# First-chunk products in plain float32, weights loaded ahead of the keys, and zero products in TensorE's idle time

## The chip, the cores and the metric

The kernel runs on one core of a Trainium2 chip. The metric is the device time of one execution in microseconds (us), the median over runs; lower is better. A profile is one further execution, seen by the hardware profiler: its span goes from the first to the last instruction.

## What is computed

A packed attention in float32 (8 batches, 8 heads, 576 positions, 64 columns a head, 32 packed rows) feeds a feed-forward layer with an ELU. The weights `w_in` (512 x 2048) and `w_out` (2048 x 512) come in as float64, everything else as float32.

```python
def sm_attn(qq, kk, vv):
    s = scale * np.matmul(qq, kk.transpose(0, 1, 3, 2))
    s = s - np.max(s, axis=-1, keepdims=True)
    a = np.exp(s)
    a = a / (np.sum(a, axis=-1, keepdims=True) + 1e-09)
    return np.matmul(a, vv)
p_packed = sm_attn(p, k, v)                 # 32 rows a head
attn = sm_attn(q, p_packed, p_packed)       # 576 rows a head
x = attn.transpose(0, 2, 1, 3).reshape(B * S, H * D)
h = x @ w_in
g = np.where(h > 0.0, h, alpha * (np.exp(np.minimum(h, 0.0)) - 1.0))
return (g @ w_out).astype(np.float32)
```

## The kernel before

**Attention, for each batch.** TensorE makes the packed scores (`s1`, L443) from packed rows and keys; VectorE (DVE) takes the maximum (L453), ScalarE (ACT) the exponential with its sum (L467); TensorE transposes it (L498), multiplies it with the values (`pv`, L524) and transposes the normalised result once more (L550), which gives `ppT`, the packed rows in the layout that both later products use. Then, for each half of 288 positions, come the scores of the queries (`s2`, L569) and their softmax over 32 packed rows: two 32 x 32 transposes out of PSUM on DVE (`fold`, L577), maximum (L584), subtraction (L587), exponential on ACT (L593), sum (L597), reciprocal (L600, L603), product (L606) and the transpose back (`unfold`, L612).

**M instead of x.** Instead of x @ w_in, the kernel multiplies `ppT` with `w_in` first: `mstep` (L663) makes M, 256 rows (32 packed rows of 8 heads, in two groups) by 512 columns of d_ff, in two parts of 256 columns for batches 0 and 1, in one for the others. The hidden product (L761) is then M times the softmax `a`.

**Splits.** [...] The splits are: M (`m_hi`, cast at L246; `m_lo`, L673), `a` (`a_hi`, L246; `a_lo`, L620), the ELU result g (`g_hi`, L246; `g_lo`, L798) and the output weights (high at L310, low at L313). L246 is a helper that copies or casts on ACT or DVE. The small products of the attention and M are in unsplit float32.

**Weights.** Each of 16 blocks of `w_in` and 16 of `w_out` (128 columns, or rows, of d_ff; 512 KB as float64) is loaded into one of three raw buffers and turned into float32 with integer and float operations: on DVE L269, L284, L290, L297 and L305, on ACT L276 and L281. A `w_out` block is then split; the first eight live in `wo_a`, the others in `wo_b`, which takes the place of batch 0's temporary buffers once these are free (`home_op`, L727).

**Steps and visits.** A step is a batch, a window of its positions (256 or 320) and one block f of d_ff: the hidden product (L761, six matmuls), ELU on ACT and DVE (L768, L774, L777), the split, and the output products (L857, L858, L860), three matmuls of 512 columns for each of two or three tiles of 128 positions, accumulated in PSUM over a visit. The 13 visits of batches 0 and 1 interleave batches and chunks of four blocks, so that few weights are needed early: steps 0 to 3 are batch 0's first window with blocks 0 to 3, steps 4 to 7 its second window, 8 to 11 batch 1's first (320 positions; three tiles a step, one of which takes 64 positions kept from batch 0), 12 to 15 its second, and step 16 is the first with block 4. Later batches run all 16 blocks at once.

**The order of the work.** Nothing is ordered by hand. `op` records each operation with a priority (mostly the step that needs it, less a lead), its cost on the engines that may do it, the operations it depends on and the buffers it takes or uses. `schedule` (L150 to L197) then plays the program with these costs: in planned time, the operation of the lowest priority number that is ready, has its buffers and finds its engine idle goes next. What is written out is that order, and each engine's queue is then in order, SP's queue of loads too. Priorities come from `T_ATT` (later batches), `T_ATT1` (batch 1), `T_S2` (the second half of batch 0), `LI` and `LO` (leads of the weights), `LM` and `TM` (M) and `LOOK` (how many steps the output products follow the hidden ones). PSUM is eight banks, held one by one or in aligned pairs (`Banks`, L101); s1, transposes, pv, s2 and M take pairs; hidden products and accumulators take single ones. At most two hidden products are open at a time (ring `h`), and keys, values and queries of later batches share two buffers in `kvq`.

Batch 0 loads first (packed rows 64 KB, keys 1152 KB, values 1152 KB, queries 1152 KB), then the first two blocks of `w_in` and one of `w_out`.

Of the kernel before, what the change touches and what calls it, by code (L numbers as in the profile page):

```python
# [20 lines left out]
def packed_attention_elu_ffn(  # L21
# [128 lines left out]
    def schedule():  # L150
# [19 lines left out]
        while todo:  # L170
# [21 lines left out]
            else:  # L192
# [3 lines left out]
                now = min(ends)  # L196
        return out  # L197

# [19 lines left out]
    warm = const.tile([P, 1], F32, name="warm")  # L218
    nc.scalar.activation(out=warm, in_=ebias, func=AF.Exp, scale=0.0)
    w_in_sb = const.tile([P, NPAIR, DFF], F32, name="w_in_sb")  # L220
    wo_a = const.tile([P, NFA, 2, E], F32R, name="wo_a")
# [7 lines left out]
    R = {k: Ring(n) for k, n in dict(  # L229
        kvq=2, m=NFC, m_late=1, a=2, tmp=3, g=3, e=2, part=2, h=2,  # L230
        raw=3, ex=2, sg=1, mi=2, p=2, ppT=3, pp=1,
    ).items()}
    R["psum"] = Banks(8)

    def banks(n):
        b = Buf(R["psum"], lambda: psum[:, b.at, :] if n == 1 else psum[:, b.at:b.at + n, :], n)
        return b

    def wo(f, part):
# [8 lines left out]

    w_ready, conv_ops = {}, []

    def weights(f, first, prio):
# [47 lines left out]
        def product(e):  # L299
            ms, pw = mi_b.t.bitcast(F32), ex_b.t.bitcast(BF16)  # L300
            out = ms
            if first:
                out = w_in_sb[:, :, f * P:(f + 1) * P]
                ms, pw = (x.rearrange("p (c f) -> p c f", c=NPAIR) for x in (ms, pw))
            nc.vector.scalar_tensor_tensor(  # L305
                out=out, in0=ms, scalar=2.0 ** -20, in1=pw, op0=ALU.mult, op1=ALU.mult
            )

        def high(e):
            copy(e, wo(f, 0), mi_b.t.bitcast(F32))  # L310

        def low(e):
            nc.vector.tensor_tensor(  # L313
                out=wo(f, 1), in0=mi_b.t.bitcast(F32), in1=wo(f, 0).bitcast(F32), op=ALU.subtract
            )
# [7 lines left out]
        g = op(prio, {"DVE": 0.42}, signed, [p, s], use=[ex_b, sg_b])  # L323
        last = op(prio, {"DVE": 0.69}, product, [w, g], use=[mi_b, ex_b])
        if not first:
# [15 lines left out]
    def attention(b, ts):  # L341
# [216 lines left out]
        st.ppT_op = op(ts[3], {"ACT": 0.27, "DVE": 0.29}, tr2c, [o], use=[pt2, st.ppT])  # L558
        st.a_done = []
        prev = []  # L560
        for half in range(2):
            ps = banks(2)
            t1, t2 = temp(), temp()
            mx, sm = {}, {}
# [45 lines left out]

            def unfold(e, t1=t1, t2=t2):
                nc.vector.transpose(out=flat(t2), in_=flat(t1))  # L612

            def hi(e, half=half, t2=t2):
                copy(e, st.a.t[0][:, :, half * HS:(half + 1) * HS],
                     flat(t2).rearrange("p (g s) -> p g s", g=G))

            def lo(e, half=half, t2=t2):
                cs = slice(half * HS, (half + 1) * HS)
                nc.vector.tensor_tensor(  # L620
                    out=st.a.t[1][:, :, cs], in0=flat(t2).rearrange("p (g s) -> p g s", g=G),
                    in1=st.a.t[0][:, :, cs].bitcast(F32), op=ALU.subtract,
                )
# [11 lines left out]
            o = op(t, {"DVE": 0.75}, smul, [o], use=[t1])  # L635
            o = op(t, {"DVE": 0.77}, unfold, [o], take=[t2], use=[t1])
            prev = [o]
            h = op(
                t, {"ACT": 0.67, "DVE": 0.4}, hi, [o] + st.a_done[-1:],
# [7 lines left out]
    def mstep(b, c, part, parts_, prio, deps=()):  # L647
        st = sts[b]
        if part == 0:
            late = b >= NB0 and c == 1  # L650
            st.m[c] = Buf(R["m_late" if late else "m"], lambda: tuple(
                (late_pools["m"] if late else mpool).tile([P, G, FC], F32R, tag=x, name=x)
                for x in ("m_hi", "m_lo")
            ))
        m_b = st.m[c]
# [4 lines left out]
        def mm(e):  # L660
            for pair in range(NPAIR):
                for g in range(G):
# [4 lines left out]
                    )  # L667

        def hi(e):
            copy(e, m_b.t[0][:, :, fs], ps.t[:, :, :w])  # L670

        def lo(e):
            nc.vector.tensor_tensor(  # L673
                out=m_b.t[1][:, :, fs], in0=ps.t[:, :, :w], in1=m_b.t[0][:, :, fs].bitcast(F32),
                op=ALU.subtract,
            )
# [3 lines left out]
        if part:  # L680
            pre.append(st.m_done[c, part - 1])
        o = op(prio, {"PE": 1.0 / parts_ + 0.03}, mm, pre, take=[ps] + ([m_b] if part == 0 else []),
               use=[st.ppT] + ([m_b] if part else []), mode=1)
        h = op(
            prio, {"ACT": 1.02 if parts_ == 1 else 0.58}, hi, [o],
            use=[ps, m_b],
        )
# [31 lines left out]
    for b in range(B):  # L719
# [6 lines left out]
        sts[b] = attention(b, ts)  # L726
    home_op = op(-1000, {"CTL": 0.0}, end_tmp0, sts[0].a_done)  # L727
    for f in range(NF):
# [14 lines left out]
    for i, (b, win, f) in enumerate(order):  # L743
# [10 lines left out]
        ))  # L754
        long = n_tok > 2 * P

        def mm(e, st=st, ps_b=ps_b, m_b=m_b, o=o, cols=cols, n_tok=n_tok):
            n = 0
            for g in range(G):
                for x, y in ((0, 0), (0, 1), (1, 0)):  # L760
                    nc.tensor.matmul(  # L761
                        ps_b.t[:, :n_tok], lhsT=m_b.t[x][:, g, o:o + P], rhs=st.a.t[y][:, g, cols],
                        start=(n == 0), stop=(n == 3 * G - 1),
                    )
                    n += 1
# [39 lines left out]
        def sub_own(e, sub=sub, e_b=e_b, own=own, n_own=n_own):  # L805
# [15 lines left out]
        x4 = op(i, {"DVE": 0.485 if n_own > 256 else 0.415}, elu_own, [x3], use=[e_b, ps_b, h_b])  # L821
        last = []
# [6 lines left out]
        if odd_half:  # L829
# [4 lines left out]
            taker["g"] = y  # L834
            z = op(i, {"DVE": 0.22}, sub_half, [y], use=[g_b])
            half_free[b - 1, f] = [y, z]
            last, taken = [z], []
        y = op(
            i, {"ACT": 0.46 if n_own > 256 else 0.4, "DVE": 0.33 if n_own > 256 else 0.29}, cast,
            [x4] + last, take=taken, use=[e_b] + ([] if taken else [g_b]),  # L840
            after=[taker["g"]] if taken else [],
        )
        taker.update(h=x1, e=x2, g=taker["g"] if odd_half else y)
        z = op(i, {"DVE": 0.48 if n_own > 256 else 0.42}, sub_own, [y], use=[e_b, g_b])
        last.append(z)
# [15 lines left out]

        prev_out = op(
            i + LOOK, {"PE": 0.693 * n_t}, out_mm,
            last + [w_ready[False, f], prev_out],
            take=acc if first else [], use=[g_b] + ([] if first else acc),
        )
        if final:
            t0 = b * S + cols.start
# [63 lines left out]
```

## Time and profile before

| | |
|---|---|
| median of 3 runs | 743.91 us (742.9 to 745.06) |
| profiled execution, its own time | 744.71 us |
| its span | 742.9 us |
| TensorE (PE) busy | 706.4 us, 95% of the span |
| weight loads on TensorE (PEld) | 568.4 us, 77% |
| DVE busy | 512.4 us, 69% |
| ACT busy | 394.5 us, 53% |
| GpSimd (POOL) busy | 19.5 us, 3% |
| mean granted TensorE clock | 0.991 |

The profile lists what each engine did and when, for groups of instructions by source line, and what ended each idle time (the releaser, after an arrow). An operation is written as output tile, arrow, input tiles. Ends of matmuls are modelled and overlap, so the distance between two starts is the better measure in a dense stream. The chain of waits is followed back from the last instruction. The stretches give the busy time of each engine between two moments.

### The profile page before, as it was taken

How to read it: one execution, taken by the hardware profiler on the slowest of the kernel's cores; microseconds unless marked ns; L12 is line 12 of the kernel's file. 1: busy time of each engine (PE TensorE's matmuls, PEld its weight loads, DVE VectorE, ACT ScalarE, POOL GpSimd, SP SyncE). 2: the span in 40 equal slices, each digit the busy share in tenths (PEclk: the TensorE clock that was granted, in tenths of full speed). 3: DMA queues.
4: the chain of work that ended last, by engine and by line, in shares of the span. 5: the costliest groups of instructions: out<-in, count | busy, mean ns of one | idle time of the engine just before them, and what ended most of it. 6: DMA issues, size and time to landing. Idle time of an engine off the chain costs nothing.

```text
span 742.9 us, 13528 instructions
## 1 busy us (share of the span) xinstructions
PE 706.4 (95%) x5144; PEld 568.4 (77%) x5144; DVE 512.4 (69%) x1276; ACT 394.5 (53%) x920; POOL 19.5 (3%) x27
## 2 busy tenths in 40 slices
PE   4649999999999999999999999999999999999997
PEld 3327777788778886788868877888777887788886
DVE  2998999986967558844686559655596549754454
ACT  3566888877654355544464346444364445444342
POOL 0000001111002000000000000000000000000000
PEclk9969999999999999999999999999999999999999
DMA  8640846675525024200511031000411011000010
GB/s 304 223 175 29 274 148 171 157 180 99 131 30 66 6 93 133 65 28 1 175 41 53 1 104 57 1 30 26 139 76 64 29 35 60 1 29 1 1 43 29
DMA packets 29361, 61.43 MB, mean 83 GB/s; under 512 B 2544, under 2 KB 11760, under 8 KB 29040
## 3 DMA queue, kind: packets, MB, share of 16 engines
q1 hardware_dynamic: 26272, 55.06, 22.0%
q0 software_dynamic: 3024, 5.51, 5.4%
q8 instruction: 40, 0.66, 0.4%
q14 instruction: 25, 0.20, 0.1%
HBM read 45.61 MB, written 14.94 MB: 82 GB/s over the span
## 4 chain that ended last, share of the span: by engine, by line
PE 88%; DVE 4%; DMA 4%; ACT 3%; issue 1%; SPq 0%; ACTq 0%
PE psum L761 27%; PE psum L857 18%; PE psum L858 17%; PE psum L860 17%; PE psum L663 4%; PE psum L524 2%; DMA kvq<-in_qT 2%; PE psum L443 1%; PE psum L498 1%; PE psum L569 1%; DMA kvq<-in_kT 1%; DMA k<-in_kT 1%; DMA out<-part 1%; DVE tmp L606 0%; ACT e L774 0%
## 5 line engine op out<-in xcount | busy, mean ns | idle before, releaser
L768 ACT ACTIVATE e<-psum 128x256 f32<-128x256 f32 (+1 forms) x256 | 104.9, 410 | 240.2 <-PE psum L761 224.4
L777 DVE SCALAR_TENSOR_TENSOR e<-e,psum 128x256 f32<-128x256 f32 (+1 forms) x256 | 110.4, 432 | 149.9 <-ACT e L774 149.8
L761 PE MATMUL psum<-a_hi,m_hi 128*128 128x320 f32 (+1 forms) x512 | 156.4, 305 | 3.9 <-ACT a_hi L246 1.3
L761 PE MATMUL psum<-a_lo,m_hi 128*128 128x320 f32 (+1 forms) x512 | 152.4, 298 | 0.4 <-DVE a_lo L620 0.4
L761 PE MATMUL psum<-a_hi,m_lo 128*128 128x320 f32 (+1 forms) x512 | 152.2, 297 | 0.0
L798 DVE TENSOR_TENSOR g_lo<-e,g_hi 128x256 fp32r<-128x256 f32 (+1 forms) x256 | 111.7, 438 | 18.2 <-ACT g_hi L246 5.7
L761 PEld LDWEIGHTS psum<-a_hi,m_hi 128*128 128x128 f32 x512 | 97.4, 190 | 27.4 <-issue 3.7
L857 PE MATMUL psum<-wo_a,g_hi 128*128 128x512 f32 x288 | 115.6, 401 | 1.6 <-DVE e L777 1.3
L774 ACT ACTIVATE e<-e 128x256 f32<-128x256 f32 (+1 forms) x256 | 113.5, 445 | 6.0
L857 PE MATMUL psum<-wo_b,g_hi 128*128 128x512 f32 x288 | 115.8, 402 | 0.0
L858 PE MATMUL psum<-wo_a,g_hi 128*128 128x512 f32 x288 | 114.0, 396 | 0.0
L858 PE MATMUL psum<-wo_b,g_hi 128*128 128x512 f32 x288 | 113.9, 395 | 0.0
L761 PEld LDWEIGHTS psum<-a_lo,m_hi 128*128 128x128 f32 x512 | 97.7, 191 | 9.1 <-DVE a_lo L620 0.6
L761 PEld LDWEIGHTS psum<-a_hi,m_lo 128*128 128x128 f32 x512 | 97.7, 191 | 0.0
L860 PE MATMUL psum<-wo_b,g_lo 128*128 128x512 f32 x288 | 87.9, 395 | 0.0
L860 PE MATMUL psum<-wo_a,g_lo 128*128 128x512 f32 x288 | 87.3, 393 | 0.0
L857 PEld LDWEIGHTS psum<-wo_a,g_hi 128*128 128x128 f32 x288 | 54.8, 190 | 19.2 <-ACT e L768 5.8
L857 PEld LDWEIGHTS psum<-wo_b,g_hi 128*128 128x128 f32 x288 | 54.2, 188 | 16.7 <-issue 3.5
L860 PEld LDWEIGHTS psum<-wo_b,g_lo 128*128 128x128 f32 x288 | 54.0, 188 | 13.1
L860 PEld LDWEIGHTS psum<-wo_a,g_lo 128*128 128x128 f32 x288 | 54.4, 189 | 12.2
L858 PEld LDWEIGHTS psum<-wo_a,g_hi 128*128 128x128 f32 x288 | 54.7, 190 | 7.5
L858 PEld LDWEIGHTS psum<-wo_b,g_hi 128*128 128x128 f32 x288 | 54.3, 189 | 7.5
(72 smaller groups left out, 705.3 us busy)
## 6 DMA issues: line engine op xcount, KB each, us to landing
out<-part SPq DMA_DIRECT2D x36, 256.0 KB, 2.3
kvq<-in_v SPq DMA_DIRECT2D x16, 512.0 KB, 4.9
raw<-in_w_in SPq DMA_DIRECT2D x16, 512.0 KB, 4.1
raw<-in_w_out SPq DMA_DIRECT2D x16, 512.0 KB, 4.1
kvq<-in_kT SPq DMA_DIRECT2D x14, 576.0 KB, 4.3
kvq<-in_qT SPq DMA_DIRECT2D x14, 576.0 KB, 5.2
out<-part POOLq DMA_DIRECT2D x21, 256.0 KB, 4.8
k<-in_kT SPq DMA_DIRECT2D x1, 1152.0 KB, 5.4
```

The lines of the kernel that those rows point to most:

```text
L443: nc.tensor.matmul(ps1[g].t[cols_of(pair), half, :HS], lhsT=p_b.t[rows_of(g), pair, :], rhs=keys(pair)[rows_of(g), half * HS:(half + 1) * HS],
L498: nc.tensor.transpose(out=pt.t[:n, c // 4, (c % 4) * P:(c % 4 + 1) * P], in_=flat(e1)[:, c * P:c * P + n], identity=ident,)
L524: nc.tensor.matmul(ps.t[cols_of(pair), g, :D], lhsT=e1T[g].t[:n, c, cols_of(pair)], rhs=values(c, h)[:n], start=(c == 0), stop=(c == NKC - 1),
L663: nc.tensor.matmul(ps.t[cols_of(pair), g, :w], lhsT=st.ppT.t[rows_of(g), pair, :], rhs=w_in_sb[rows_of(g), pair, c * FC + part * w:c * FC ...
L761: nc.tensor.matmul(ps_b.t[:, :n_tok], lhsT=m_b.t[x][:, g, o:o + P], rhs=st.a.t[y][:, g, cols], start=(n == 0), stop=(n == 3 * G - 1),)
L768: nc.scalar.activation(out=e_b.t[:, :n_tok], in_=ps_b.t[:, :n_tok], func=AF.Relu, scale=-1.0)
L774: nc.scalar.activation(out=x, in_=x, func=AF.Exp, scale=-1.0)
L777: nc.vector.scalar_tensor_tensor(out=out, in0=e_b.t[:, cs], scalar=-1.0, in1=ps_b.t[:, cs], op0=ALU.add, op1=ALU.max)
L798: nc.vector.tensor_tensor(out=g_b.t[1][:, cs], in0=x, in1=g_b.t[0][:, cs].bitcast(F32), op=ALU.subtract)
L857: nc.tensor.matmul(a.t, lhsT=g_b.t[0][:, t], rhs=wo(f, 0), start=first, stop=False)
L858: nc.tensor.matmul(a.t, lhsT=g_b.t[0][:, t], rhs=wo(f, 1), start=False, stop=False)
L860: nc.tensor.matmul(a.t, lhsT=g_b.t[1][:, t], rhs=wo(f, 0), start=False, stop=final)
```

## The change

- **Priorities and leads.** `T_ATT`, `T_ATT1`, `LI`, `LM`, `LOOK`, `TM` and `T_S2` get new numbers.
- **Loads.** The first four blocks of `w_in` get load priorities ahead of batch 0's keys (-60 to -57, keys -46), and the first two of `w_out` stand between its values (-45) and its queries (-43).
- **Unsplit float32.** For batches 0 and 1 and the first four blocks, the hidden product (`h_whole`) multiplies M and `a` in float32, two matmuls over the two groups instead of six; `a` is written whole into `st.af`, which lies in the place of the keys and queries of batch 0, and only later split (`T_AS`) for the other blocks. M's first chunk is only copied, in float32. In the output product (`g_whole`), the ELU is written straight into g in float32, and one float32 matmul of 512 columns for each tile, with unsplit weights kept in `w_words`, takes the place of three. These four `w_out` blocks are split later (`T_WS`). `home_op` waits for the sixteen hidden products that read `st.af`.
- **M's buffers.** The high and low parts of M become buffers of their own rings.
- **Zeros.** A PSUM bank is held from the start to the hidden product of the fifth step (`FILL_END`). After planning, `filled` puts in front of each TensorE operation up to there as many matmuls of a bfloat16 zero tile (128 x 128 by 256 columns) as make 0.7 of the planned idle time before it, at 0.107 us each.

```diff
-    T_ATT, T_ATT1 = [12, 13.5, 14.5, 15.5, 17, 17], [-12, -11, -9, -8, -7, -6]
-    LI, LO, LM, LOOK = 5, 3, 3, 2.5
-    TM = [24.5, 24.5, 28.5, 28.5]
-    T_S2, STAY, SWITCH = -1, 4, 0.12
+    T_ATT, T_ATT1 = [12, 14.0, 15.0, 16.0, 17.5, 17.5], [-12, -11, -11, -10, -10, -9]
+    LI, LO, LM, LOOK = 4.5, 3.0, 2.5, 3.5
+    TM = [24.5, 24.5, 28.0, 28.0]
+    T_S2, STAY, SWITCH = 0, 4, 0.12
+    F_PLAIN, H_PLAIN = 4, [0, 1]
+    T_WS, T_AS = 20, 6
+    FILL_END, FILL = 4, 0.7
...
-        return out
+        return filled(out)
+    def filled(out):
+        pe = [o for o, e in out if e == "PE"]
+        fill, free = {}, 1.0
+        for o in pe:
+            if any(u.end is not None and u.end < o.start for u in fill_b.users[1:]):
+                break
+            fill[id(o)] = int(FILL * (o.start - free) / 0.107)
+            free = o.start + o.on["PE"]
...
+    def zeros(e):
+        nc.tensor.matmul(fill_b.t[:, :2 * P], lhsT=zero[:, :P], rhs=zero, start=True, stop=True)
+    fill_b = banks(1)
+    op(-1000, {"CTL": 0.0}, lambda e: None, take=[fill_b])
...
-        ld = op(prio - 8, {"DMA": 1.45}, load, take=[raw])
+        ld = op(-60 + f if first and f < 4 else -44 + f / 9 if f < 2 else prio - 8, {"DMA": 1.45}, load, take=[raw])
...
+        if plain:
+            h = op(T_WS + f, {"ACT": 0.61}, high, [last], use=words_b)
+            w_split[f] = op(T_WS + f, {"DVE": 0.69}, low, [h], use=words_b)
+        elif not first:
...
+        whole = b in H_PLAIN
+        if whole:
+            x = ("k0", "q0")[b]
+            st.af = Buf(R[x], lambda x=x: tmp0.tile([P, NPAIR, S], F32, tag=x, name=x))
...
+            st.af_done.append(o)
+            if whole:
+                t = first_use["b", b] + T_AS
             h = op(
                 t, {"ACT": 0.67, "DVE": 0.4}, hi, [o] + st.a_done[-1:],
...
-        st.m_done[c, part] = op(
-            prio, {"DVE": 1.2 if parts_ == 1 else 0.68}, lo, [h], use=[ps, m_b]
-        )
+        st.m_done[c, part] = h
+        if not whole:
+            st.m_done[c, part] = op(
+                prio, {"DVE": 1.2 if parts_ == 1 else 0.68}, lo, [h], use=[ps] + m_b
+            )
...
+        h_whole, g_whole = b in H_PLAIN and c == 0, b < NB0 and f < F_PLAIN
...
+            if h_whole:
+                for g in range(G):
+                    nc.tensor.matmul(
+                        ps_b.t[:, :n_tok], lhsT=m_b[0].t[:, g, o:o + P].bitcast(F32),
+                        rhs=st.af.t[:, g, cols], start=(g == 0), stop=(g == G - 1),
+                    )
+                return
...
+        cost = (1.07 if long else 0.87) if h_whole else (0.885 if long else 0.714)
+        if i == FILL_END:
+            fill_b.users.append(x1)
+        if h_whole:
+            home_op.deps.append(x1)
...
+            if g_whole:
+                for t, a in zip(ts, acc):
+                    nc.tensor.matmul(
+                        a.t, lhsT=g_b.t[0][:, t].bitcast(F32), rhs=w_words[f // 2].t[:, f % 2, :],
+                        start=first, stop=final,
+                    )
+                return
...
-            i + LOOK, {"PE": 0.693 * n_t}, out_mm,
+            i + LOOK, {"PE": (0.9 if g_whole else 0.693) * n_t}, out_mm,
```

More of the change, by code (lines that the diff above doesn't have):

```diff
@@ L229, in packed_attention_elu_ffn @@
     R = {k: Ring(n) for k, n in dict(
-        kvq=2, m=NFC, m_late=1, a=2, tmp=3, g=3, e=2, part=2, h=2,
-        raw=3, ex=2, sg=1, mi=2, p=2, ppT=3, pp=1,
+        kvq=2, m_hi=NFC, m_lo=NFC, m_hi_late=1, m_lo_late=1, a=2, tmp=3, g=3, e=2, part=2, h=2,
+        raw=3, ex=2, sg=1, mi=2, p=2, ppT=3, pp=1, k0=1, q0=1,
     ).items()}
@@ L246, in copy @@
         (nc.scalar.copy if e == "ACT" else nc.vector.tensor_copy)(out=out, in_=in_)
-    w_ready, conv_ops = {}, []
+    w_ready, w_split, conv_ops = {}, {}, []
+    w_words = [
+        Buf(R["m_lo"], lambda: mpool.tile([P, 2, E], F32, tag="m_lo", name="w_words"))
+        for _ in range(F_PLAIN // 2)
+    ]
     def weights(f, first, prio):
@@ L323, in weights @@
         g = op(prio, {"DVE": 0.42}, signed, [p, s], use=[ex_b, sg_b])
-        last = op(prio, {"DVE": 0.69}, product, [w, g], use=[mi_b, ex_b])
-        if not first:
+        words_b = w_words[f // 2:f // 2 + 1] if plain else []
+        take = words_b if f % 2 == 0 else []
+        last = op(
+            prio, {"DVE": 0.69}, product, [w, g], take=take,
+            use=[mi_b, ex_b] + [b for b in words_b if b not in take],
+            after=[w_ready[False, f - 1]] if words_b and f % 2 else [],
+        )
+        if plain:
+            h = op(T_WS + f, {"ACT": 0.61}, high, [last], use=words_b)
+            w_split[f] = op(T_WS + f, {"DVE": 0.69}, low, [h], use=words_b)
+        elif not first:
             home = [home_op] if f >= NFA else []
@@ L562, in attention @@
             ps = banks(2)
-            t1, t2 = temp(), temp()
+            t1, t2 = temp(), st.af if whole else temp()
             mx, sm = {}, {}
@@ L635, in attention @@
             o = op(t, {"DVE": 0.75}, smul, [o], use=[t1])
-            o = op(t, {"DVE": 0.77}, unfold, [o], take=[t2], use=[t1])
+            take = [] if whole and half else [t2]
+            o = op(t, {"DVE": 0.77}, unfold, [o], take=take, use=[t1] + ([] if take else [t2]))
             prev = [o]
+            st.af_done.append(o)
+            if whole:
+                t = first_use["b", b] + T_AS
             h = op(
@@ L650, in mstep @@
             late = b >= NB0 and c == 1
[L651 to L654, printed above, removed]
+            st.m[c] = [Buf(
+                R[x + "_late" if late else x],
+                lambda x=x: (late_pools["m"] if late else mpool).tile([P, G, FC], F32R, tag=x, name=x),
+            ) for x in (("m_hi",) if b in H_PLAIN and c == 0 else ("m_hi", "m_lo"))]
         m_b = st.m[c]
@@ L667, in mm @@
                     )
+        whole = b in H_PLAIN and c == 0
         def hi(e):
-            copy(e, m_b.t[0][:, :, fs], ps.t[:, :, :w])
+            out = m_b[0].t[:, :, fs]
+            copy(e, out.bitcast(F32) if whole else out, ps.t[:, :, :w])
         def lo(e):
             nc.vector.tensor_tensor(
-                out=m_b.t[1][:, :, fs], in0=ps.t[:, :, :w], in1=m_b.t[0][:, :, fs].bitcast(F32),
+                out=m_b[1].t[:, :, fs], in0=ps.t[:, :, :w], in1=m_b[0].t[:, :, fs].bitcast(F32),
                 op=ALU.subtract,
@@ L681, in mstep @@
             pre.append(st.m_done[c, part - 1])
-        o = op(prio, {"PE": 1.0 / parts_ + 0.03}, mm, pre, take=[ps] + ([m_b] if part == 0 else []),
-               use=[st.ppT] + ([m_b] if part else []), mode=1)
+        o = op(prio, {"PE": 1.0 / parts_ + 0.03}, mm, pre, take=[ps] + (m_b if part == 0 else []),
+               use=[st.ppT] + (m_b if part else []), mode=1)
         h = op(
-            prio, {"ACT": 1.02 if parts_ == 1 else 0.58}, hi, [o],
-            use=[ps, m_b],
-        )
-        st.m_done[c, part] = op(
-            prio, {"DVE": 1.2 if parts_ == 1 else 0.68}, lo, [h], use=[ps, m_b]
-        )
+            prio, {"ACT": 1.02 if parts_ == 1 else 0.58} | ({"DVE": 0.69} if whole else {}), hi, [o],
+            use=[ps] + m_b,
+        )
+        st.m_done[c, part] = h
[3 more added lines that the diff above has]
+            )
         st.m_parts = parts_
@@ L726, in packed_attention_elu_ffn @@
         sts[b] = attention(b, ts)
-    home_op = op(-1000, {"CTL": 0.0}, end_tmp0, sts[0].a_done)
+    home_op = op(
+        -1000, {"CTL": 0.0}, end_tmp0,
+        sts[0].af_done + [x for b in range(NB0) if b == 0 or b in H_PLAIN for x in sts[b].a_done],
+    )
     for f in range(NF):
@@ L834, in packed_attention_elu_ffn @@
             taker["g"] = y
[L835 to L841, printed above, removed]
-        )
+            half_free[b - 1, f] = [y]
+            if not g_whole:
+                z = op(i, {"DVE": 0.22}, sub_half, [y], use=[g_b])
+                half_free[b - 1, f] = [y, z]
+            last, taken = half_free[b - 1, f][-1:], []
+        into = dict(take=taken, use=[] if taken else [g_b], after=[taker["g"]] if taken else [])
+        x4 = op(
+            i, {"DVE": 0.485 if n_own > 256 else 0.415}, elu_own, [x3] + (last if g_whole else []),
+            take=into["take"] if g_whole else [], after=into["after"] if g_whole else [],
+            use=[e_b, ps_b, h_b] + (into["use"] if g_whole else []),
+        )
+        y = z = x4
+        if not g_whole:
+            y = op(
+                i, {"ACT": 0.46 if n_own > 256 else 0.4, "DVE": 0.33 if n_own > 256 else 0.29}, cast,
+                [x4] + last, take=into["take"], use=[e_b] + into["use"], after=into["after"],
+            )
+            z = op(i, {"DVE": 0.48 if n_own > 256 else 0.42}, sub_own, [y], use=[e_b, g_b])
         taker.update(h=x1, e=x2, g=taker["g"] if odd_half else y)
-        z = op(i, {"DVE": 0.48 if n_own > 256 else 0.42}, sub_own, [y], use=[e_b, g_b])
         last.append(z)
@@ L862, in packed_attention_elu_ffn @@
         prev_out = op(
-            i + LOOK, {"PE": 0.693 * n_t}, out_mm,
-            last + [w_ready[False, f], prev_out],
+            i + LOOK, {"PE": (0.9 if g_whole else 0.693) * n_t}, out_mm,
+            last + [w_split.get(f) if not g_whole and f < F_PLAIN else w_ready[False, f], prev_out],
             take=acc if first else [], use=[g_b] + ([] if first else acc),
         )
+        if g_whole:
+            w_words[f // 2].users.append(prev_out)
         if final:
```

64 lines of the change are left out of this document (40 added, 24 removed).

## The prediction, made before the run

> **What bounds the kernel now.** I read the stretches first: TensorE's busy time by stage tells where time can be had at all. Columns: stretch and length, then busy time of PE, PEld, DVE, ACT and POOL with instruction counts, granted clock, DMA share, GB/s.
>
> ```profile
> 0.00:52.95 52.95, 26.84 (x376) 15.69 (x377) 36.53 (x83) 27.77 (x59) 0.69 (x6) 0.92 0.70 241
> 52.95:71.28 18.33, 17.05 (x89) 13.97 (x89) 15.93 (x39) 10.67 (x26) 0.00 (x0) 0.87 0.12 45
> 71.28:160.00 88.72, 85.14 (x575) 68.17 (x575) 82.55 (x204) 75.09 (x180) 6.38 (x7) 1.00 0.63 182
> 160.00:742.90 582.90, 577.32 (x4108) 470.52 (x4106) 377.36 (x953) 280.93 (x659) 12.42 (x14) 1.00 0.19 54
> ```
>
> Of 36.5 us without TensorE work, 26.1 lie before 52.95, 1.3 up to 71.28, 3.6 up to 160 and 5.6 in all the rest. From 160 on TensorE is the bound, so the edits to `T_ATT`, `LOOK` and `TM` there can gain 5.6 at most; they reorder work that DVE (377 busy of 583) and ACT cover, and I cost them at nothing. If that cover failed, each wait would cost its length. What can be had is at the start. Next, TensorE's own timeline there (start, length, line, count, idle before and its releaser).
>
> ```profile
> 6.71 2.18 PE L443 MATMUL psum<-k,p 64*32 64x288 f32 x32 [6.71 <-DMA k<-in_kT]
> ...
> 17.40 2.17 PE L569 MATMUL psum<-q,ppT 64*32 64x288 f32 x32 [0.35 <-ACT ppT L246]
> ...
> 48.11 1.21 PE L569 MATMUL psum<-kvq,ppT 64*32 64x288 f32 x16 [6.92 <-DVE m_lo L673]
> 50.47 0.55 PE L761 MATMUL psum<-a_hi,m_hi 128*128 128x256 f32 x1 [1.14 <-ACT ex L276]
> ...
> 52.95 0.58 PE L761 MATMUL psum<-a_hi,m_hi 128*128 128x256 f32 x1 [0.86 <-DVE e L777]
> ...
> 71.28 0.42 PE L761 MATMUL psum<-a_hi,m_hi 128*128 128x320 f32 x1 [1.28 <-ACT a_hi L246]
> ```
>
> The keys come at 6.71, the queries' products at 17.40, and steady work only at 52.95. The row at 71.28 is the ninth step (step 8, first of batch 1), my mark below: it waited for batch 1's second softmax, copied on ACT and still to be split on DVE. And why was DVE late?
>
> ```profile
> 14.40 0.43 DVE L269 TENSOR_SCALAR ex<-raw 128x512 uint16<-128x512 uint16 x1 [2.32 <-DMA raw<-in_w_in]
> ...
> 18.70 0.48 DVE L577 STREAM_TRANSPOSE tmp<-psum 128x288 f32<-128x288 f32 x1 [0.27 <-PE psum L569]
> ...
> 28.62 0.77 DVE L612 STREAM_TRANSPOSE tmp<-tmp 128x576 f32<-128x576 f32 x1
> ```
>
> It converts no weight before 14.40, though it has little else to do until then, and afterwards the softmax of the first half (18.70 to 29.39, 10.7 us) shares it with weights. So DVE bounds the start.
>
> **The change, part by part.** *Loads.* Three weight blocks (512 KB each) go ahead of the keys, a fourth and two output blocks ahead of the queries, all on SP's queue. Keys, values and queries are all moved back; stores and POOL's queue start later than that. The rate:
>
> ```profile
> 7.00:14.40 7.40, 5.22 (x74) 3.21 (x62) 2.07 (x6) 3.14 (x8) 0.00 (x0) 1.00 1.04 378
> ```
>
> At 378 GB/s three blocks (1.57 MB) are 4.2 us: keys at 10.9. In the kernel before, the queries follow the keys by 2.36 MB, 6.2 us: 12.9, hidden since they are used at 17.40. With six blocks (3.15 MB, 8.3 us) ahead they land at 21.2, and that cover is gone. The way from keys to queries took 17.40 - 6.71 = 10.7 at the slow clock, hence 21.6 at most: queries and chain arrive together, and I take 21.3. Of the 10.7 us of the first half's softmax, seven weight instructions between its own (0.4 to 0.7 each) are about 3.3, which will have been done: 7.4. So the first hidden product can start at 21.3 + 0.6 + 7.4 = 29.3 us; the ends are 27.5 (next to nothing in between) and 32.6 (10.7 again). The fourth weight load waits on the queue for one of three raw buffers, with the values queued behind it; DVE frees one some 2 us after the first block lands, before the keys are in, so I cost that at nothing; a late buffer would delay the values by as much.
>
> *Less for DVE.* The rows of what is dropped or deferred, up to 71.3 us (count, then busy and mean ns):
>
> ```profile
> L620 DVE TENSOR_TENSOR a_lo<-tmp,a_hi 128x576 fp32r<-128x576 f32 x4 | 3.0, 754 | 0.1
> ...
> L798 DVE TENSOR_TENSOR g_lo<-e,g_hi 128x256 fp32r<-128x256 f32 x7 | 2.8, 404 | 0.6 <-ACT g_hi L246 0.6
> L305 DVE SCALAR_TENSOR_TENSOR w_in_sb<-mi,ex 128x512 f32<-128x512 f32 x4 | 2.7, 676 | 0.0
> L673 DVE TENSOR_TENSOR m_lo<-psum,m_hi 128x512 fp32r<-128x512 f32 x4 | 2.7, 675 | 0.0
> L313 DVE TENSOR_TENSOR wo_a<-mi,wo_a 128x512 fp32r<-128x512 f32 x4 | 2.7, 671 | 0.0
> ```
>
> Leaving L305 aside (it stays), 3.0 + 2.8 + 2.7 + 2.7 = 11.2 us go. DVE was busy 36.53 + 15.93 = 52.5 us before 71.28; 41.3 are left. With the first block in at about 4.6, and the idle time it had between 14.40 and 71.28 (56.9 less some 50.2 busy, 6.7) kept, DVE allows step 8 at 52.6.
>
> *More for TensorE.* The sixteen first steps use unsplit float32. Rows of the chain of waits (start, length, line, count) price it:
>
> ```profile
> 147.97 1.13 PE psum L443 x32
> ...
> 178.54 1.39 PE psum L524 x80
> ...
> 187.80 1.14 PE psum L569 x32
> ...
> 196.40 0.89 PE psum L761 x6
> 198.69 0.88 PE psum L761 x6
> 200.96 1.02 PE psum L663 x16
> ...
> 236.89 0.73 PE psum L761 x6
> ...
> 451.96 1.88 PE psum L663 x32
> ```
>
> Now: 320 columns 0.88, 256 columns 0.73, and between two steps 2.27 - 0.88 = 1.39 for two output tiles, 0.695 each. L663 is unsplit float32 on quarter-width tiles: 16 instructions over 512 columns take 1.02, 32 take 1.88, so a dense 512 columns are 0.86, 1.68 ns a column. Then an output tile is 0.86 (+0.165), a hidden product of 256 columns twice 0.43 (+0.13), of 320 columns 1.075 (+0.195). Ends: 1.99 ns a column (1.02 over 512, nothing overlapped) and no extra at all; I take 1.68, as a stream of steps is dense. Steps 0 to 7: 4 x (0.86 + 1.72) + 4 x (1.075 + 1.72) = 21.5 (17.6 to 25.5). Steps 8 to 15, with 20 tiles: 20 x 0.165 + 4 x 0.195 + 4 x 0.13 = +4.6 (0 to +9.3).
>
> [...]
>
> *Step 8.* TensorE also has to do batch 1's values and queries (1.39 + 1.14), its transposes (no row here; 1.4, an estimate by the values' row) and four parts of M at 0.47: 5.8. For the ELUs of the first steps I keep the 1.14 + 0.86 = 2.0 that stood at 50.47 and 52.95. Step 8 then starts at 29.3 + 21.5 + 5.8 + 2.0 = 58.6 instead of 71.28: -12.7. DVE's 52.6 hides behind that.
>
> *After it.* DVE's 82.55 us get the deferred splits (+3.0 + 2.7) and lose the ELU splits of eight steps (8 x 0.404 = -3.2): 85.1, while TensorE's time grows by 4.6. DVE has more room, so of the 3.6 us of waits I let 1.0 go (3 go at best, 2 come at worst).
>
> *Zeros.* They are 0.7 of the planned idle time, counted at 0.107 us each. The trace has no such product. The nearest are six of 256 columns in 0.73, 0.12 each; at the slow clock (L443: 2.18 at 6.71, 1.13 at 147.97, 1.9 times) 0.23. The planner's costs put the keys' products at 3 x 1.45 + 3.3 + 2.2 = 9.85, so 0.7 x 8.85 / 0.107 = 57 zeros stand ahead of them. The clock: the granted rows say little here (0.92 for a stretch in which L443 runs 1.9 times too long), so I go by durations. If the zeros run slow for 5 us and then at 0.12, they are done by 11 us, about when the keys land: nothing.
>
> [...]
>
> **Sum.** -12.7 + 4.6 - 1.0 = -9.1 us. The span of 742.9 becomes 733.8. The profiled execution took 744.71, 1.8 beside its span and 0.8 above the median; on the median of 743.91 it is 734.8.
>
> **The rivals.** *Better:* no wait for ELUs (step 8 at 56.6) and 2 us less of later waits: -14.7 + 4.6 - 2.0 = -12.1, 731.8. For it: DVE would allow 52.6. Against it: b1's softmax outranks the ELUs in the planner.
>
> *A bank in place of the split.* The zeros hold one of eight PSUM banks until the fifth step, and attention, M and scores take pairs. That such a wait is real, TensorE's waits show:
>
> ```profile
> PE psum L569 <- DVE m_lo L673: 6.9, 1, 6.9
> ```
>
> There the queries' products stood behind `m_lo`, which freed their pair. The change frees it by the copy, but has three pairs, not four. If one such wait comes back whole: step 8 at 65.5, -5.8 + 4.6 = -1.2, 742.7. It decides once two single banks are held besides.
>
> *Slower: zeros in the way.* TensorE takes its queue in order. Above 0.107 / 0.7 = 0.153 us each, zeros outlast the gaps they were counted from. At 0.23, some 20 us of planned gaps (8.85 ahead of the keys and, by my estimate, 11 of the 18 from there to 29.3) would hold 130 zeros, 30 us: 10 too many. Batch 1's 4.8 us at 1.9 times are 4.5 more. Step 8 at 73.1: +1.8 + 4.6 = +6.4, 750.3. For it: every row of attention before 35 us is slow. Against it: after the long gap at 48.11 dense work did bring the clock back (0.58 for 256 columns at 52.95, 0.42 for 320 at 71.28). Here the change would not do what it says.
>
> **How the numbers follow.** Forecast 0.60, better 0.17, bank 0.13, zeros 0.10. A measurement of this kernel can tell about 0.3%, 2.2 us, from no change: 741.7 and 746.1. Faster: 0.55 of the forecast's 0.60, 0.17, and 0.04 of the bank's: 0.76. Same: 0.05 + 0.08 = 0.13. Slower: 0.10 and 0.01 of the bank's: 0.11. The range runs from below the better case, as the float32 may cost less, 729.5, past the bank's case to 743.5, where the dear end of float32 (4.7 more from steps 8 to 15, 4.0 more ahead of step 8) also lands.
>
> **What would show it.** Right: first weight instruction on DVE near 5 us, keys' products near 11 and at 1.1 us, first hidden product near 29, output tiles at 0.86, step 8 near 59, and the last stretch unchanged. Wrong: zeros over 0.153 us with TensorE busy on them when an operand is ready; queries' products waiting for a bank; tiles near 1.0; or step 8 past 66.

## The result, and the profile after

The changed kernel takes 730.93 us (median of 4 runs, 730.79 to 731.63); the kernel before, beside it, 744.48. The ratio is 0.9821 with a 95% interval of 0.9801 to 0.9842: 1.8% faster, 13.55 us between the medians. The forecast was 734.8 within 729.5 to 743.5. The profiled execution took 730.94, its span is 728.9, 14.0 less than before.

TensorE's timeline of the changed kernel (start, length, engine, line, tiles, count, idle before and its releaser):

```profile
1.09 7.69 PE L262 MATMUL psum<-zero 128*128 128x256 bf16 x57 [1.09 <-DVE zero L241]
10.25 1.21 PE L500 MATMUL psum<-k,p 64*32 64x288 f32 x32 [1.47 <-DMA k<-in_kT]
11.39 2.69 PE L262 MATMUL psum<-zero 128*128 128x256 bf16 x23
...
21.95 0.72 PE L626 MATMUL psum<-q,ppT 64*32 64x288 f32 x16 [0.30 <-ACT ppT L276]
...
31.85 1.03 PE L836 MATMUL psum<-k,m_hi 128*128 128x256 f32 x4
...
37.25 1.88 PE L955 MATMUL psum<-w_words,g_hi 128*128 128x512 f32 x4
38.97 1.03 PE L836 MATMUL psum<-k,m_hi 128*128 128x256 f32 x4
39.84 1.88 PE L955 MATMUL psum<-w_words,g_hi 128*128 128x512 f32 x4
41.82 0.72 PE L626 MATMUL psum<-kvq,ppT 64*32 64x288 f32 x16
43.38 0.72 PE L626 MATMUL psum<-kvq,ppT 64*32 64x288 f32 x16 [0.84 <-DMA kvq<-in_qT]
44.03 1.34 PE L836 MATMUL psum<-k,m_hi 128*128 128x320 f32 x4
...
61.90 2.32 PE L836 MATMUL psum<-q,m_hi 128*128 128x320 f32 x8
...
65.18 1.34 PE L836 MATMUL psum<-q,m_hi 128*128 128x320 f32 x4 [0.96 <-DVE g_hi L859]
66.36 2.74 PE L955 MATMUL psum<-w_words,g_hi 128*128 128x512 f32 x6
68.94 2.10 PE L836 MATMUL psum<-q,m_hi 128*128 128x320 f32 x8
70.88 2.74 PE L955 MATMUL psum<-w_words,g_hi 128*128 128x512 f32 x6
```

L262 are the zeros, L836 the unsplit hidden products, L955 the unsplit output products; where they are split, each operand is a high part (a cast to float32r) and a low part (the float32r difference), and three products, high x high, high x low and low x high, stand in the place of one. The keys' products start at 10.25, the queries' at 21.95, the first hidden product at 31.85, the first output at 37.25 (54.4 before), step 8 at 61.90 (71.28 before). From 37.25 on nearly nothing is left open. Two output tiles last from 37.25 to 38.97: 0.86 each. Three last from 66.36 to 68.94: 0.86 again.

VectorE's first weight instruction, and TensorE's stretches (columns as in the prediction):

```profile
4.60 0.43 DVE L304 TENSOR_SCALAR ex<-raw 128x512 uint16<-128x512 uint16 x1 [3.56 <-DMA raw<-in_w_in]
```

```profile
0.00:61.90 61.90, 56.88 (x632) 35.78 (x633) 53.15 (x124) 40.68 (x85) 0.70 (x6) 1.00 0.75 264
61.90:160.00 98.10, 97.02 (x594) 71.93 (x593) 87.09 (x207) 81.04 (x193) 8.13 (x9) 1.00 0.58 153
160.00:728.90 568.90, 563.47 (x4015) 462.15 (x4013) 366.09 (x932) 264.64 (x623) 10.50 (x12) 1.00 0.19 53
```

The first 61.90 us count the zeros (21.2 us of them) as busy. After step 8 TensorE is idle for 1.1 us until 160 (3.6 before), and 5.4 later (5.6 before). A second mark is useful: the last add of batches 0 and 1 into the output, which GpSimd issues. First of the kernel before, then of the changed one:

```profile
238.65 0.86 POOL L881 DMA_DIRECT2D out<-part  x1 [4.41 <-DVE part L246]
```

```profile
226.24 0.86 POOL L987 DMA_DIRECT2D out<-part  x1 [2.92 <-ACT part L276]
```

12.4 of the 14.0 us are won by then, and 1.6 afterwards, where no product changed its form.

Of the 9.4 us by which step 8 comes earlier, 3.1 are won ahead of the first hidden product (31.85; before, the first row below) and 6.3 behind it. Part of these 6.3 is the clock. Behind its wait of 6.92, which ends at 48.11, the kernel before runs at half speed until about 57.4 (granted clock 0.50 from 48.11 to 57.40, 1.00 from 61.00 to 71.28), 0.43 from one output product to the next, then 0.23, which costs some 3 us by an estimate from these distances. The changed kernel, without that wait, has full speed there (granted clock 1.00 from 37.25 to 61.90, 0.86 an output tile at 37.25 as at 66.36). The rows of the kernel before:

```profile
34.96 0.58 PE L761 MATMUL psum<-a_hi,m_hi 128*128 128x256 f32 x1
...
54.40 0.63 PE L857 MATMUL psum<-wo_a,g_hi 128*128 128x512 f32 x1
54.83 0.63 PE L858 MATMUL psum<-wo_a,g_hi 128*128 128x512 f32 x1
...
57.74 0.39 PE L857 MATMUL psum<-wo_a,g_hi 128*128 128x512 f32 x1
57.97 0.39 PE L858 MATMUL psum<-wo_a,g_hi 128*128 128x512 f32 x1
```

### The profile page after: what moved, and what is told of

Same layout as the page of the kernel before. It is cut to its first block, busy times and chain, and to the rows that moved or that the text cites. A ratio compares the mean times of both kernels' runs of the same rounds, so it can differ in the third digit from the quotient of the medians.

```text
span 728.9 us, 13737 instructions
## 1 busy us (share of the span) xinstructions
PE 717.4 (98%) x5238; PEld 569.9 (78%) x5238; DVE 506.3 (69%) x1259; ACT 386.4 (53%) x898; POOL 19.3 (3%) x27
## 4 chain that ended last, share of the span: by engine, by line
PE 92%; DMA 3%; DVE 3%; SPq 0%; ACT 0%; issue 0%; ACTq 0%
PE psum L843 27%; PE psum L961 17%; PE psum L962 17%; PE psum L964 17%; PE psum L729 4%; PE psum L955 3%; DMA kvq<-in_qT 2%; PE psum L836 2%; PE psum L581 1%; DMA raw<-in_w_out 1%; PE psum L626 1%; PE psum L555 1%; PE psum L500 1%; DVE mi L325 1%; DMA raw<-in_w_in 1%; DVE ex L304 0%
## 5 line engine op out<-in xcount | busy, mean ns | idle before, releaser
L843 PE MATMUL psum<-a_hi,m_hi 128*128 128x256 f32 (+1 forms) x480 | 147.3, 307 | 0.1
L843 PE MATMUL psum<-a_lo,m_hi 128*128 128x256 f32 (+1 forms) x480 | 141.9, 296 | 0.0
L843 PE MATMUL psum<-a_hi,m_lo 128*128 128x256 f32 (+1 forms) x480 | 141.9, 296 | 0.0
L961 PE MATMUL psum<-wo_b,g_hi 128*128 128x512 f32 x288 | 115.3, 400 | 0.0
L843 PEld LDWEIGHTS psum<-a_hi,m_hi 128*128 128x128 f32 x480 | 90.3, 188 | 27.3 <-issue 10.7
L961 PE MATMUL psum<-wo_a,g_hi 128*128 128x512 f32 x252 | 99.4, 394 | 0.0
L962 PE MATMUL psum<-wo_a,g_hi 128*128 128x512 f32 x252 | 99.3, 394 | 0.0
L843 PEld LDWEIGHTS psum<-a_lo,m_hi 128*128 128x128 f32 x480 | 90.6, 189 | 9.2 <-issue 1.0
L843 PEld LDWEIGHTS psum<-a_hi,m_lo 128*128 128x128 f32 x480 | 90.5, 189 | 0.0
L964 PE MATMUL psum<-wo_a,g_lo 128*128 128x512 f32 x252 | 76.1, 392 | 0.0
L276 DVE CAST g_hi<-e 128x256 fp32r<-128x256 f32 (+1 forms) x184 | 55.2, 300 | 12.2 <-PE psum L962 3.7
L961 PEld LDWEIGHTS psum<-wo_b,g_hi 128*128 128x128 f32 x288 | 54.2, 188 | 10.9 <-issue 3.2
L961 PEld LDWEIGHTS psum<-wo_a,g_hi 128*128 128x128 f32 x252 | 47.5, 188 | 9.4 <-ACT g_hi L276 2.5
```

What stands on the lines that cost most here:

```text
L276: (nc.scalar.copy if e == "ACT" else nc.vector.tensor_copy)(out=out, in_=in_)
L843: nc.tensor.matmul(ps_b.t[:, :n_tok], lhsT=m_b[x].t[:, g, o:o + P], rhs=st.a.t[y][:, g, cols], start=(n == 0), stop=(n == 3 * G - 1),)
L962: nc.tensor.matmul(a.t, lhsT=g_b.t[0][:, t], rhs=wo(f, 1), start=False, stop=False)
L964: nc.tensor.matmul(a.t, lhsT=g_b.t[1][:, t], rhs=wo(f, 0), start=False, stop=final)
```

## The experiments

The theories: the prediction's, that VectorE bounds the start and is relieved (the *VectorE* theory, later divided into *loads*, the early weights, and *relief*, the splits left out); and as rivals the *clock* (the zeros do it), the *order* (the new priorities do it), the *bank* and *zeros in the way*. All times are medians, with the ratio to the kernel before on the same chip; the last add is that of the one profiled execution, which in e3 and e5 was 1.9 and 1.8 us above the median and in e8 1.6 below it.

| run | time, us | ratio (95% interval) | last add, us |
|---|---|---|---|
| changed kernel | 730.93 | 0.9821 (0.9801 to 0.9842) | 226.24 |
| e1 no zeros | 730.34 | 0.9827 (0.9803 to 0.9850) | 226.58 |
| e2 old load order | 738.25 | 0.9931 (0.9910 to 0.9953) | 234.66 |
| e3 all split | 732.56 | 0.9855 (0.9833 to 0.9876) | 231.76 |
| e4 old priorities | 733.22 | 0.9856 (0.9835 to 0.9877) | 228.16 |
| e5 loads alone, on the kernel before | 739.06 | 0.9936 (0.9916 to 0.9956) | 234.13 |
| e6 hidden product unsplit only | 730.04 | 0.9811 (0.9788 to 0.9833) | 227.01 |
| e7 output product unsplit only | 759.28 | 1.0203 (1.0185 to 1.0220) | 255.61 |
| e8 no zeros, no bank | 729.11 | 0.9800 (0.9774 to 0.9826) | 223.89 |
| e9 changed kernel again | 731.17 | 0.9837 (0.9819 to 0.9856) | 226.94 |
| e10 hidden product only, no zeros, no bank | 730.57 | 0.9828 (0.9810 to 0.9847) | 226.84 |
| e11 two banks held | 730.45 | 0.9830 (0.9811 to 0.9848) | 227.01 |
| e12 zeros doubled | 745.02 | 1.0015 (1.0002 to 1.0028) | 241.52 |

**e1, no zeros.**

```diff
-    FILL_END, FILL = 4, 0.7
+    FILL_END, FILL = 4, 0.0
```

Expected: 

> The changed kernel (730.9) without a single zero product; the bank stays held. VectorE theory (the start is bound by VectorE and by when it gets its first weights; zeros only shorten the products of the attention): the products between keys and queries run at half clock, some 3 us more until the queries' products, the first steps at half clock add about 2, so step 8 moves from 61.9 to some 66 and the time is 735 (733 to 737). Clock theory (the released clock is what brings the gain): most of the 13.5 us goes, 740 or more.

Measured 730.34: the zeros bring nothing, and both theories had the number wrong, the clock theory by far. TensorE's timeline without zeros shows why:

```profile
10.94 2.17 PE L500 MATMUL psum<-k,p 64*32 64x288 f32 x32 [10.94 <-DMA k<-in_kT]
...
22.33 1.21 PE L626 MATMUL psum<-q,ppT 64*32 64x288 f32 x16 [0.36 <-ACT ppT L276]
...
33.53 2.70 PE L836 MATMUL psum<-k,m_hi 128*128 128x256 f32 x8
...
43.28 1.20 PE L626 MATMUL psum<-kvq,ppT 64*32 64x288 f32 x32
44.41 1.34 PE L836 MATMUL psum<-k,m_hi 128*128 128x320 f32 x4
...
62.28 2.32 PE L836 MATMUL psum<-q,m_hi 128*128 128x320 f32 x8
```

The keys' products do take 2.17 instead of 1.2 us and the first hidden product comes 1.7 us later, at 33.53. But at 43.28 the queries of batch 1 have landed, for which the changed kernel stood still from 42.54 to 43.38, and both kernels are within 0.4 us of each other from there to step 8 and to the last add. The zeros shorten work ahead of a wait for a load. The clock comes without them too, with the work itself: the hidden products at 44.41 take 1.34, as in the changed kernel. So e1 shows what the zeros are worth, not what the clock is worth.

**e2, the old load order.**

```diff
-        ld = op(-60 + f if first and f < 4 else -44 + f / 9 if f < 2 else prio - 8, {"DMA": 1.45}, load, take=[raw])
+        ld = op(prio - 8, {"DMA": 1.45}, load, take=[raw])
```

Expected: 

> The changed kernel with the load priorities of before: keys, values and queries first, then weights. VectorE theory: the first weight instruction falls back from 4.6 to some 14 us, VectorE loses about 8 us of work in otherwise idle time, step 8 moves from 61.9 to some 68, time 737 (734 to 740). Clock theory: keys 4 us earlier, nothing lost, 729 to 732.

Measured 738.25: 7.3 us more, as the VectorE theory had it. VectorE's first weight instruction, and TensorE at the first outputs:

```profile
13.72 0.43 DVE L304 TENSOR_SCALAR ex<-raw 128x512 uint16<-128x512 uint16 x1 [2.46 <-DMA raw<-in_w_in]
```

```profile
31.82 1.99 PE L836 MATMUL psum<-k,m_hi 128*128 128x256 f32 x8
...
43.27 6.51 PE L262 MATMUL psum<-zero 128*128 128x256 bf16 x58
50.51 1.99 PE L836 MATMUL psum<-k,m_hi 128*128 128x256 f32 x8 [0.74 <-DVE g_hi L859]
52.34 1.88 PE L955 MATMUL psum<-w_words,g_hi 128*128 128x512 f32 x4
54.06 1.24 PE L836 MATMUL psum<-k,m_hi 128*128 128x320 f32 x4
55.13 1.88 PE L955 MATMUL psum<-w_words,g_hi 128*128 128x512 f32 x4
```

```profile
50.08 0.38 DVE L859 SCALAR_TENSOR_TENSOR g_hi<-e,psum 128x256 f32<-128x256 f32 x1
```

The first hidden products come at 31.82, as early as in the changed kernel, but the first ELU (the row of VectorE just above) runs at 50.08 and the first output at 52.34, not 37.25: VectorE, 9 us behind, has weights and batch 1's softmax to do first. Most of TensorE's wait is filled with 58 zeros (43.27), which no list of waits counts; only 0.74 is left as a wait. Step 8 starts at 65.23, not at 68, but with five output steps behind it instead of eight. That is how late weights cost time here.

**e3, all products split.**

```diff
-    F_PLAIN, H_PLAIN = 4, [0, 1]
+    F_PLAIN, H_PLAIN = 0, []
```

Expected: 

> The changed kernel with all products split as before (no block and no batch in unsplit float32). VectorE theory: 11.2 us of VectorE work come back ahead of step 8, TensorE has 4 us less there and 4.6 us less in steps 8 to 15; step 8 at about 69, waits after it come back in part, 734 (731 to 737). Clock theory: TensorE is relieved of some 9 us and nothing is lost, 722 to 727.

Measured 732.56, within the range of the VectorE theory and against the clock theory. The two forms are nearly even: beside everything else in the change, unsplit float32 is worth 1.6 us by the medians, and the intervals of the two ratios overlap. Step 8 comes at 64.26, not at 69, with the same seven output steps and four parts of M behind it as in the kernel before at 71.28: 7.0 us earlier, with every hidden and output product split.

**e4, the old priorities.**

```diff
-    T_ATT, T_ATT1 = [12, 14.0, 15.0, 16.0, 17.5, 17.5], [-12, -11, -11, -10, -10, -9]
-    LI, LO, LM, LOOK = 4.5, 3.0, 2.5, 3.5
-    TM = [24.5, 24.5, 28.0, 28.0]
-    T_S2, STAY, SWITCH = 0, 4, 0.12
+    T_ATT, T_ATT1 = [12, 13.5, 14.5, 15.5, 17, 17], [-12, -11, -9, -8, -7, -6]
+    LI, LO, LM, LOOK = 5, 3, 3, 2.5
+    TM = [24.5, 24.5, 28.5, 28.5]
+    T_S2, STAY, SWITCH = -1, 4, 0.12
```

Expected: 

> The changed kernel with the priorities, leads and lags of before (T_ATT, T_ATT1, LI, LM, LOOK, TM, T_S2). VectorE theory: the same work in another order; ELUs wait a little longer before step 8, 733 (731 to 736). Order theory (the new numbers bring the gain): 737 or more.

Measured 733.22: 2.3 us by the medians, again with overlapping intervals. The order theory, as the one cause of the gain, falls. The marks place what there is: the last add comes 1.9 us later than in the changed kernel, and behind it the span runs on for 503.4 us (731.6 - 228.2) against 502.7.

**e5, the new load order alone, on the kernel before.** The edit is the first line of e2, on the kernel before.

Expected: 

> The kernel before (743.9) with the new load order alone, everything else as it was. Loads theory (what brings the gain is that VectorE gets weights at 4.6 instead of 14.4 us): 735 to 738, most of the gain of the whole change. Relief theory (the prediction's: what VectorE no longer splits is the larger part, 11.2 us of its time before step 8): 739 to 742.

Measured 739.06, 5.2 us faster, between the two ranges. e2 has everything but the loads and wins 5.2 as well. The two sum to 10.4 of the 12.5 to 13.55 of the whole: the parts help each other somewhat. At step 8 the loads alone do most: it starts at 65.57 with eight output steps and four parts of M behind it, 5.7 us earlier and one output step (1.4) ahead. The profiled execution keeps only 3.9 of these 7.1 us in its span. With early weights but all the splits, TensorE waits for ELUs (first row of its waits shown) and again for batch 1's loads:

```profile
PE psum L761 <- DVE e L777: 4.0, 3, 1.8
PE psum L443 <- DMA kvq<-in_kT: 2.8, 1, 2.8
PE psum L569 <- DMA kvq<-in_qT: 1.7, 1, 1.7
```

The longest of the waits for ELUs ends at 46.87 and another, of 1.80, at 70.04. From 71.11 on TensorE runs at half speed for about 4 us (0.27 for a split product of 320 columns, instead of 0.15), a loss that stands in no list of waits.

**e6, only the hidden product unsplit.**

```diff
-    F_PLAIN, H_PLAIN = 4, [0, 1]
+    F_PLAIN, H_PLAIN = 0, [0, 1]
```

Expected: 

> The changed kernel (730.9) with unsplit float32 in the hidden product alone; ELU results and output weights are split in all steps. TensorE gets back 36 output tiles at 0.165 to 0.18, some 6 us; VectorE gets the splits of four weight blocks (2.7) and of sixteen steps (about 7) back. Loads theory (after the early weights VectorE has time to spare and TensorE is the bound): 725 to 729. Relief theory: 732 to 736.

Measured 730.04, between both ranges. Of the 6 us that TensorE gets back, 3.6 are lost until 160 in waits for ELUs, against 1.0 in the changed kernel (at 65.18); where the rest goes is open:

```profile
PE psum L836 <- DVE e L859: 1.8, 1, 1.8
PE psum L843 <- DVE e L859: 1.8, 2, 1.1
```

So beside the rest of the change the unsplit output product is worth nothing that these runs can tell, and relieving TensorE alone does not shorten the time.

**e7, only the output product unsplit.**

```diff
-    F_PLAIN, H_PLAIN = 4, [0, 1]
+    F_PLAIN, H_PLAIN = 4, []
```

Expected: 

> The changed kernel with unsplit float32 in the output product alone; M and the softmax are split in all steps, the splits of the softmax before its first use. TensorE gets back some 2.5 us of hidden products, VectorE gets m_lo (2.7) back and a_lo (3.0) early. Loads theory: 729 to 731. Relief theory: 734 to 737.

Measured 759.28, 28 us slower than the changed kernel, foreseen by nobody, and no measure of the product's form. One wait makes most of it:

```profile
PE psum L729 <- ACT tmp L524: 21.7, 2, 21.3
```

```profile
112.28 1.11 PE L729 MATMUL psum<-w_in_sb,ppT 64*32 64x256 f32 x16 [21.31 <-ACT tmp L524]
```

M's product (L729) stands at the head of TensorE's queue for 21.3 us, until the exponential of batch 2's attention (L524) has read its scores out of PSUM. The scores themselves were made at 86.14 to 87.27, but VectorE works off weights until 109.89, when it takes the maximum on which the exponential waits. That M wanted the PSUM pair of these scores is what this wait suggests; that a different choice of order would remove it was not tried.

**e8, no zeros and no bank held for them.**

```diff
-    FILL_END, FILL = 4, 0.7
+    FILL_END, FILL = 4, 0.0
...
-    op(-1000, {"CTL": 0.0}, lambda e: None, take=[fill_b])
```

Expected: 

> The changed kernel without zeros and without the PSUM bank held for them. If the held bank costs anything, this is faster than the same kernel with the bank held (730.3) by 1 to 3 us; if the bank is free of cost, it is 730 to 731 again.

Measured 729.11, the lowest median of all. Its ratio of 0.9800 lies just below the intervals of e1 and of the changed kernel (from 0.9803 and 0.9801), but its own, 0.9774 to 0.9826, overlaps both, so a gain of 1 to 2 us is possible and not shown.

**e9 to e12 on one chip.** The changed kernel again, as a measure. Expected: 

> The changed kernel once more, on the chip of the three runs beside it, as their measure: 730 to 732.

Measured 731.17.

**e10, what the runs left of the change**, is e8 with the line of e6. Expected: 

> Unsplit float32 in the hidden product alone, no zeros and no bank held: the parts of the change that the runs showed to be worth something. Loads theory (loads, hidden product and priorities bring it, zeros and output product nothing): 728 to 731, at or below the changed kernel. If zeros or the unsplit output product are needed after all when both are missing: 733 or more.

Measured 730.57, the same as the changed kernel on that chip. Zeros, bank and unsplit output product can go at no loss, and there is no gain in leaving them out either.

**e11, a second bank held.**

```diff
+    bank_c = banks(1)
+    op(-1000, {"CTL": 0.0}, lambda e: None, take=[bank_c])
...
             fill_b.users.append(x1)
+            bank_c.users.append(x1)
```

Expected: 

> The changed kernel with a second PSUM bank held up to the fifth step. Bank rival (a pair less makes attention and M wait at the start): 734 to 738. If banks are not short there: 731 to 732.

Measured 730.45: banks are not short up to the fifth step, the bank rival falls.

**e12, twice the zeros.**

```diff
-    FILL_END, FILL = 4, 0.7
+    FILL_END, FILL = 4, 1.4
```

Expected: 

> The changed kernel with 1.4 instead of 0.7 of the planned idle time in zeros. Zeros-in-the-way rival: at 0.107 to 0.117 us each they outlast the planned gaps of some 25 us by 0.4 to 0.5 of them, TensorE comes 8 to 10 us late to the fifth step, less what its waits for loads take up: 736 to 741. If the start is VectorE's pace alone: 731 to 733.

Measured 745.02, 13.9 more than e9 and above the rival's range. TensorE's timeline with twice the zeros:

```profile
1.09 15.41 PE L262 MATMUL psum<-zero 128*128 128x256 bf16 x115 [1.09 <-DVE zero L241]
16.43 1.20 PE L500 MATMUL psum<-k,p 64*32 64x288 f32 x32
17.56 5.20 PE L262 MATMUL psum<-zero 128*128 128x256 bf16 x46
...
31.93 0.71 PE L626 MATMUL psum<-q,ppT 64*32 64x288 f32 x16
...
77.22 2.32 PE L836 MATMUL psum<-q,m_hi 128*128 128x320 f32 x8
```

Keys that are there at 11.3 (issued at 2.59, landed 8.7 us later) wait for the zeros until 16.43, 5.1 us; the row has no idle time and no releaser. The delay grows through the attention (31.93 for the queries, ten late) and step 8 is 15.3 late. It is 14.6 to 15.3 at the last add and 13.9 by the medians, so little of it is given back. There are 115 + 46 and so on, 336 zeros in all against 162. So the mechanism of the rival is real, and it is the dose of 0.7 that keeps it away.

## Why the prediction was right, and where its sizes were off

**VectorE bounds the start, and early weights move it: shown.** e2 and e5 switch the loads from both sides, 7.3 and 5.2 us. The prediction had the first weight at 4.6 (4.60), the keys' products at 10.9 (10.25), the queries' at 21.3 (21.95).

**The first hidden product: 29.3 forecast, 31.85 found.** The softmax of the first half was put at 7.4 us, since no weights would stand between. It took from 22.77 to 31.56, 8.8 us: output weights took the place of the others on VectorE. That and 0.65 of the queries are most of the 2.6.

**Float32's price: right.** A tile is 0.86 as forecast, 256 columns 0.87 (38.97 to 39.84), 320 columns 1.07 in e2 (54.06 to 55.13; 1.18 where other work has just ended, 44.03 to 45.21). Steps 8 to 15 then cost 20 x 0.165 + 4 x 0.19 + 4 x 0.14 = 4.6 us more, as forecast.

**Step 8: 58.6 forecast, 61.90 found, and the term beside it was mis-sized.** From 31.85 it took 30.0 us, where 21.5 + 5.8 + 2.0 = 29.3 was forecast; the late start is what made it late. That the two lengths agree is in part luck: two of the four parts of M and most of the transposes came before 31.85, the 2.0 for ELUs do not stand as waits, and in their place are two parts of M that were not counted (0.60 each, where 0.47 was forecast for a part), 1.3 of zeros and 0.84 of waiting for queries. But "Step 8 then starts at 58.6 instead of 71.28: -12.7" compares marks with different work behind them. At 71.28 the kernel before had seven output steps and four parts of M done (14 and 64 instructions of its lines L857 and L663), the changed one at 61.90 eight and six. That is one output step, 1.4, and two parts, 1.2: 2.6 us ahead that the sum did not count.

**After it: -1.0 forecast, -2.5 found in waits until 160.** VectorE had room, as argued, and had by 61.90 taken eleven weight blocks through L325 and begun the twelfth, where the kernel before had done eight by 71.28 (L290).

**The sum of the spans.** Step 8 -9.4, work ahead -2.6, float32 +4.6, waits -2.5: -9.9 of the -12.4 at the last add. The other 2.5 stand in no wait of TensorE, whose ends are modelled. Some 0.6 of them are again work behind the mark: 148 output tiles against 150 and about 70 hidden products against 69 (instructions of L955 and L961, of L857, and of L836, L843 and L761). The rest stays open. Behind the last add are 1.6 more. So the forecast of -9.1 missed the -14.0 by 4.9, and would have missed by more if the late step 8 (+3.3) had not gone the other way. Behind the last add the priorities were costed at nothing. e4, with the old ones, loses 2.7 in its profiled execution, of which 1.9 by the last add; the kernels with the new priorities take 500.6 to 502.7 us from there on, the three with the old ones (before, e4, e5) 503.4 to 504.9. So beside the rest of the change the priorities are worth some 2 us, spread over the whole. What of it lies behind 160 is within the 5.6 that the prediction allowed, and each difference is near what a run can tell.

**Relief: its worth depends on what stands beside it.** The prediction counted the 11.2 us less for VectorE as a bound only (52.6, hidden behind TensorE); the expectation of e5 made it the larger part. e3 gives it all back and loses 1.6, since TensorE is relieved at the same time. But taking one part away at a time hides parts that can stand in for each other. With the loads alone (e5) the ratio is 0.9936. Unsplit float32 and zeros added to that, with the old priorities, give 0.9856 (e4); new priorities and zeros added, with all splits, give 0.9855 (e3). Each is some 6 us, clear of the intervals, while both together give 0.9821. So relief and order can largely stand in for each other, or else the zeros, which are in both and worth nothing in the whole change (e1), bring part of each 6 us: the loads with the zeros alone were not tried, nor were M's separate buffers.

**Rivals.** The bank, as a cost of several us, fell with e11; 1 to 2 us of it stay possible (e8). The zeros in the way did not come, as a zero takes 0.107 to 0.117 us (23 from 11.39 to 14.08), under the 0.153 of the prediction; e12 passed the point by the count instead and paid 13.9. The better case gave 731.8, near the result, but by other terms: step 8 came at 61.90 and not at 56.6. Its first condition, no wait for ELUs before step 8, nearly held: TensorE's waits there are keys 1.5, the zero tile 1.1, queries 0.8, and three smaller ones of attention, and the zeros from 35.61 to 36.28 can hide at most 0.7 of one for the first ELU (it ends at 35.79). Its second, 2 us less of later waits, came true (2.5). The zeros, costed at nothing, were worth nothing in the whole change: e1. The clock itself was worth some 3 us behind 48.11, by the estimate above, and there it came behind dense work: 0.43 an output product at 54.40, 0.23 at 57.74.

## What to carry to other kernels

Look first at what an engine that will be the bound does while the first loads are on their way: here new priorities for six weight loads were worth 5.2 us alone and 7.3 beside the rest, while the work taken off that engine was worth 1.6 beside the rest. Such a number holds for what stands beside it: parts that can stand in for each other look small when they are taken away one at a time, so add them one at a time as well. When work moves from one nearly full engine to another, price both sides in their stretch; 11 us less on VectorE ahead of step 8 stood against some 8.5 more on TensorE in sixteen steps. When two marks of two traces are compared, count the work behind each of them, and before filling idle time to keep a clock, ask which load ends the next wait.

## What the runs showed of the hardware

- Behind products of zeros TensorE ran at full speed: the keys' products take 1.14 us there (10.25 to 11.39), without zeros (e1) 2.17. The 57 first zeros took 7.5 us from start to start (the row's 7.69 has the last one's modelled end); at 0.107 each they would be 6.1, so about 13 ran at half speed (421 ns each in the records, 272 later), some 3 us. The 5 that the prediction allowed was its author's estimate.
- Behind a gap of 2 us it was gone again. Where the keys came 2.07 and 2.00 us after the last zero (e3, e7), the row of their products lasts 1.98 and 1.85 us; where the gap was 0.72 to 1.47 (the changed kernel, e4, e6, e9, e11), it lasts 1.20 to 1.21.
- The granted clock showed 1.00 while products ran at half speed (0 to 40 us of the kernel before, L443 at 684 ns instead of 403); durations were the better witness there.
